# Expert results added to the token rows two at a time, and one overflow branch placed later

## The chip, the cores and the metric

The kernel runs on one core of a Trainium2 chip. The metric is the device time of one execution in microseconds (us). Before the change it is 507.67 us, the median of three runs (507.65 to 509.39).

The core has a matrix engine (PE, TensorE), with a separate row for its weight loads (PEld), a vector engine (DVE), an activation engine (ACT), GpSimd (POOL) and SyncE (SP). Each works through its own list of instructions in order and waits on semaphores. SP issues the plain transfers (DMA), POOL the indirect ones, which gather or scatter rows by a list of indices.

## The reference

Three layers follow one another on 1536 tokens of 512 numbers.

```python
# 1. attention: a band of 16 tokens to each side, and 24 block summaries per sequence -> x (1536 x 512)
# 2. mixture of 8 experts, at most one expert per token
do_compute = x @ w_skip > 0
e_idx = argmax(x[do_compute] @ w_gate); gate_w = softmax probability of e_idx
for e in range(8):                       # mask: the tokens of expert e
    y[mask] = gate_w * (relu(xc[mask] @ w1[e]) @ w2[e])
out[do_compute] = xc + y                 # the other tokens keep x
# 3. gated feed-forward layer over all tokens
gate = sigmoid(x @ w_gate2); val = x @ w_val
result = (gate * val) @ w_out
```

The tokens of an expert are known only at run time, and no token belongs to two experts.

## The kernel before

**Attention (0 to some 92 us)** writes the twelve tiles of 128 token rows to `x_d`, a table in device memory. It has 128 spare rows behind the 1536 tokens. The routing yields for each expert a list of token numbers. The attention's instructions are put in order by a planner with costs per operation; the change touches it at one place, the write of zeros into the spare rows (`("z",)`, L591).

**Experts (some 92 to 196 us).** The first 64 tokens of each expert are gathered from `x_d` into `xg` (two experts per gather, L713). For each expert e, `e_s1(e, half)` multiplies them with `w1` (L735; halves 0 and 1 use two of four weight tiles each), `e_relu` applies relu (`hs`, ACT L743 and DVE L744), `e_tr` transposes (`hTp` on PE L749, copied into `hT` by ACT L751 and DVE L752), `e_s2` multiplies with `w2` into `yp` (L768), and `e_out` scales by the gate into `ysb` (ACT L778; for the last two experts DVE L785, and ACT L784 writes the same rows into `YY`). `e_add(e)` (L791) is the indirect DMA on POOL that adds `ysb` to the token rows in `x_d`; this text calls it addition e. Slots of a list that hold no token point at spare rows. The pieces are interleaved by hand: while expert e is in `e_s1`, expert e-1 is in `e_tr` and `e_s2`.

**Overflow.** Tokens 65 to 192 of an expert have a branch of their own, `e_more(e)` (L1031): each engine loads the expert's count (`TENSOR_LOAD CNT`, L1032) and compares; if it is over 64, `o_tile` computes 128 more rows and adds them by its own indirect DMA (L899). If not, each engine jumps over that code and makes up its semaphores (L1037 for experts 0 to 5, L1043 for 6 and 7). `e_more(e)` also emits `e_s2(e)` and `e_out(e)` for experts 0 to 5; for 6 and 7 it holds the branch alone.

In between, `split_some` converts weights of the third layer piece by piece (ACT L989, L1000; DVE L987 to L1001).

**Third layer (some 196 us to the end).** SP loads tokens 0 to 511 from `x_d` into `xg` (L1104) before additions 6 and 7; the results of experts 6 and 7 for these tokens come in through a multiplication of `YY` with a one-hot matrix (`hot`, L1114, L1130). PE transposes `xg` (L1125) and adds both in `xp`; ACT and DVE split `xp` into `XH` and `XL` (L1131, L1132). Tokens 512 to 1535 are loaded after all additions (`x2t`, L1152) and transposed by `x2` (L1157). `m_s1` (L1179) and `m_s2` (L1208) are the products, 48 and 24 matrix instructions at a time. The first group of `m_s1` needs tokens 0 to 511 alone; the first `x2` transposes stand behind its first 24 instructions.

**What orders the additions.** All additions write `x_d`. The framework that tracks dependencies therefore makes each one wait for the one before, and makes the loads L1104 wait for additions 0 to 5, addition 6 for these loads, and L1152 for additions 6 and 7. POOL's DMAs take eight semaphores (`DMASW0` to `DMASW7`) in turn.

```python
        if e == E - 1:
            e_more(e - 1)          # L1057, between e_s1(7, 0) and e_tr(6)
```

Of the kernel before, what the change touches and what calls it, by code (L numbers as in the profile page):

```python
# [9 lines left out]
F32 = mybir.dt.float32  # L10
# [6 lines left out]
ALU = mybir.AluOpType  # L17
# [3 lines left out]
B, H, S, D = 2, 8, 768, 64  # L21
DM = 512
E, DF = 8, 1024
# [9 lines left out]
SLOT = 64  # L33
NOV = 11
CAP = SLOT + 128
XROWS = B * S + 128
NPT, NRE = 7, 0
LD = (19, 2)
CUT_1 = 3
# [37 lines left out]
    sm=-0.4, setup=-2.3, xw=0.2, gex=0.7, end=-0.5, xtr=-0.8, lg=-1.1, vst=0.3, ksum=0.9, pv=0.1, ex=0.1,  # L77
# [22 lines left out]
C_TOK = C_I128 + 128  # L100
C_DH = C_TOK + NT
C_DUM2 = C_DH + 1
C_DUM = C_DUM2 + 1
C_DHS = C_DUM + 1
C_DUMS = C_DHS + 1
C_ALL = C_DUMS + 1
# [8 lines left out]
def consts():  # L115
    c, a = np.zeros((128, C_ALL), np.float32), np.zeros((128, A_ALL), np.float32)
    c[:, C_ID:C_ID + 128] = np.eye(128, dtype=np.float32)
    qq = np.arange(64)[:, None]
    jj = np.arange(KW)[None, :]
    for v in range(3):  # L120
        ok = np.abs(jj - WIN - qq) < WIN
        if v == 0:
            ok &= jj >= WIN
        if v == 2:
            ok &= jj < WIN + 64
        m = np.full((64, KC), np.float32(8.0 * np.log(BLK)), np.float32)
        m[:, :KW] = np.where(ok, np.float32(0.0), np.float32(-8e9))
        a[:, A_MASK + v * KC:A_MASK + (v + 1) * KC] = np.concatenate([m, m], 0)
    for p in range(128):
        if p % 32 < 9:  # L130
            a[p, A_SEL + p % 32] = 1.0
    c[:, C_IOTA8:C_IOTA8 + 8] = np.arange(8)
    c[:, C_P] = np.arange(128)
    c[:, C_T16:C_T16 + NOV] = np.arange(NOV)
    c[:, C_TRI8:C_TRI8 + 64] = (np.arange(8)[None, :] <= np.arange(8)[:, None]).reshape(-1)
    c[:, C_THR:C_THR + 12] = CAP + 128 * np.arange(12)
    a[:, A_TRI:A_TRI + 128] = np.arange(128)[:, None] < np.arange(128)[None, :]
    a[0, A_EROW:A_EROW + 8] = -BIG
    c[:, C_I64:C_I64 + CAP] = np.arange(CAP) - BIG
    c[:, C_I128:C_I128 + 128] = np.arange(128)  # L140
    p = np.arange(128)
    c[:, C_TOK:C_TOK + NT] = 1 + p[:, None] + 128 * np.arange(NT)[None, :]
    c[:, C_DH] = p // 64 - 2
    c[:, C_DUM2] = 2 * B * S + p - (p // 64 - 2)
    c[:, C_DUM] = B * S + p + 1
    c[:, C_DHS] = -1 - p // 64
    c[:, C_DUMS] = 2 * B * S + p - (-1 - p // 64)
    return c, a


# [1 line left out]
def body(ctx: ExitStack, tc, qx, kx, vx, vtx, cst, csa, wgs, w1, w2, mgate, mval, mout, out):  # L152
    nc = tc.nc
    pe, dve, act, pool, sp = nc.tensor, nc.vector, nc.scalar, nc.gpsimd, nc.sync
    ctx.enter_context(tc.manual_schedule())
    x_d = tc.dram_tile([XROWS, DM], F32, name="x_d")
# [3 lines left out]
    C = keep.tile([128, C_ALL], F32, name="C")  # L160
# [5 lines left out]
    LS = keep.tile([128, 2 * E], F32, name="LS")  # L166
# [45 lines left out]
    Z = a1.tile([128, DM], F32, name="Z")  # L212
# [346 lines left out]
    def op(key, engine, f, *deps):  # L559
        ops[key] = (engine, COST[key[0]], f, [d for d in deps if d in ops])  # L560
# [22 lines left out]
    for b in range(B):  # L583
        for n in range(NP):
# [3 lines left out]
                op(("k", b, n), "sp", lambda b=b, n=n: load_k(b, n))  # L588
                op(("ksum", b, n), "dve", lambda b=b, n=n: ksum(b, n), ("k", b, n))
            op(("vsum", b, n), "dve", lambda b=b, n=n: vsum(b, n), ("vt", b, n))  # L590
    op(("z",), "sp", lambda: sp.dma_start(x_d[B * S:, :], Z))  # L591

    def vsums(b, *deps):
        op(("vst", b), "pe", lambda: vsum_t(b), *[("vsum", b, n) for n in range(NP)], *deps)
# [73 lines left out]
    while avail:  # L668
        best = None
        for key in avail:  # L670
            g, c, _, deps = ops[key]
            r = max((done[d] + (0.0 if ops[d][0] == g else LAT[ops[d][0]] + (LSP if g == "sp" else 0.0)) for d in deps), default=0.0)
# [4 lines left out]
        g, c = ops[key][:2]  # L677
# [27 lines left out]
    m1 = mst.enter_context(tc.tile_pool(name="m1", bufs=1, side="right"))  # L705
# [4 lines left out]
    xg = [m1.tile([128, DM], F32, name=f"xg{j}") for j in range(4)]  # L710
# [62 lines left out]
    def e_out(e):  # L773
# [13 lines left out]
        if e < E - 2:  # L787
            e_add(e)

    def e_add(e):  # L790
        pool.indirect_dma_start(  # L791
            x_h, bass.IndirectOffsetOnAxis(ap=SI[:, e:e + 1], axis=0), ysbs[e], None, compute_op=ALU.add
        )


    def o_eq(u, base, pos, p):
# [109 lines left out]
    with tc.If(nl > 0):  # L906
        with tc.For_i(0, nl, 1) as it:
# [15 lines left out]
                op=ALU.subtract,  # L923
# [33 lines left out]
        gather(j)  # L957
    dve.tensor_scalar(LI2, LS[:, E:2 * E], -1.0, 0.0, op0=ALU.add, op1=ALU.max)
    sm = m1.tile([128, E], F32, name="sm")
    dve.tensor_scalar(sm, LS[:, :E], 0.5, C[:, C_DUM2:C_DUM2 + 1], op0=ALU.is_lt, op1=ALU.mult)  # L960
    dve.scalar_tensor_tensor(sm, LS[:, :E], 2.0, sm, op0=ALU.mult, op1=ALU.add)
    dve.tensor_scalar(SI, sm, C[:, C_DH:C_DH + 1], None, op0=ALU.add)
    z = E - 1
# [55 lines left out]
    def split_some(i):  # L1019
        for _ in range(SPN[i]):  # L1020
            k = next(sp_order, None)
            if k is not None:
                next(sp0[k], None)
# [7 lines left out]
    def e_more(e):  # L1031
        rv = nc.values_load(CNT[0:1, e:e + 1], min_val=0, max_val=B * S)  # L1032
        yi, gt = SI2[:, e:e + 1], GLS[:, E + e:E + e + 1]
        if e in cuts:
            yps[e] = pB.tile([128, 512], F32, name=f"yp{e}", tag="b")
            e_s2_mm(e, range(S2N))
            with tc.If(rv > SLOT) as cmp:  # L1037
                o_tile(e, xo[e], yi, gt, cuts[e], lambda: e_s2_mm(e, range(S2N, 8)))
            with cmp.Else():
                e_s2_mm(e, range(S2N, 8))  # L1040
            e_out(e)
        else:
            with tc.If(rv > SLOT):  # L1043
                o_tile(e, xo[e], yi, gt, Cut(e, *w12(e)))
# [8 lines left out]
    for e in range(E):  # L1053
        if e + AHD < E:
            o_gather(e + AHD)
        e_s1(e, 0)
        if e == E - 1:  # L1057
            e_more(e - 1)
        if e >= 1:
            e_tr(e - 1)  # L1060
        load_to(ahead(3 * e + 1), True)
        if e == E - 2:
            split_some(1)
        e_s1(e, 1)
        if e == E - 1:
            split_some(5)
        e_relu(e)
        load_to(ahead(3 * e + 2), True)
        if e >= E - 2:
            split_some(2 if e == E - 2 else 6)  # L1070
        if e % 2 == 1 and e + 1 < E:
            g_tr((e + 1) // 2)
        if 1 <= e < E - 1:
            if e < E - 1:
                cuts[e - 1] = Cut(e - 1, *w12(e - 1), CUT_0)
                cuts[e - 1](CUT_0)
            else:
                e_s2(e - 1)
            if e == E - 2:
                split_some(3)  # L1080
            load_to(ahead(3 * e + 3), True)
            e_more(e - 1)
            if wpos >= NW:
                load_free(8 * e)
        if 8 * e >= NW > 8 * e - 8:
            xst.close()
            wpool = ctx.enter_context(tc.tile_pool(name="wpool", bufs=1, side="left"))
            rawt = ctx.enter_context(tc.tile_pool(name="rawt", bufs=RWB, side="left"))
            WHL = [(wpool.tile([128, 3072], F32R, name="wh0"), wpool.tile([128, 3072], F32R, name="wl0")), None]
        if E - 3 <= e < E - 1:  # L1090
            split_some(0 if e == E - 3 else 4)
# [9 lines left out]
    XH = [[hst.tile([128, 512], F32R, name=f"XH0_{n}", tag="wh") for n in range(4)]]  # L1101
    XL = [[hst.tile([128, 512], F32R, name=f"XL0_{n}", tag="wh") for n in range(4)]]
    for t in range(4):
        sp.dma_start(xg[t], x_d[t * 128:t * 128 + 128, :])  # L1104
    e_add(E - 2)
    TT = m1.tile([128, 2], F32, name="TT")
    dve.tensor_copy(TT[0:64, :], LS[0:64, E - 2:E])
# [40 lines left out]
    x2t = {}  # L1148

    def x2_load(t):  # L1150
        x2t[t] = z4.tile([128, DM], F32, name=f"x2t{t}", tag="x2t")
        sp.dma_start(x2t[t], x_d[t * 128:t * 128 + 128, :])  # L1152

    def x2(t):
        ps = pB.tile([128, 4, 128], F32, name=f"x2p{t}", tag="b")
# [144 lines left out]
```

## Time and profile before

| What | Value |
|---|---|
| median of three runs | 507.67 us |
| the profiled execution: its time / its span | 510.82 us / 509.0 us |
| PE busy, share of the span | 486.7 us, 96% |
| POOL busy | 107.8 us, 21% |
| chain that ended last: PE / DMA | 58% / 8% of the span |
| of it, additions `x_d<-ysb,SI` | 6% |
| granted PE clock, mean | 0.973 |

The span runs from the first to the last instruction. The chain that ended last is followed back from the last instruction: at each step to whatever released it, or to the instruction before it on its engine. PE is called busy in most slices; where it stands still is seen in the timeline, in brackets behind an instruction: the idle time before it and who ended it. Additions are counted by POOL only for the time in which it writes their descriptors (some 1.55 us); how long the data takes stands in the chain.

### The profile page before, as it was taken

What the parts mean: (1) busy time and instruction counts of PE and PEld (TensorE: products, weight loads), DVE (VectorE), ACT (ScalarE), POOL (GpSimd) and SP (SyncE); (2) the same over time, 40 slices, a digit from 0 to 9 for tenths busy, and PEclk for the clock granted to TensorE, in tenths of its full rate; (3) what the DMA queues carried; (4) which work ended last, traced back from release to release, by engine and by line L of the source; (5) the groups of instructions that cost most, each with busy time, mean ns of one, the idle gap of its engine ahead of it and who ended that gap; (6) DMA issues with size and microseconds to landing.
All of it is one profiled execution on the core that took longest, in us unless ns stands there. A gap on an engine that the chain in (4) does not pass through costs nothing.

```text
span 509.0 us, 8116 instructions
## 1 busy us (share of the span) xinstructions
PE 486.7 (96%) x2889; PEld 371.7 (73%) x2889; DVE 287.2 (56%) x813; ACT 187.2 (37%) x403; POOL 107.8 (21%) x158
## 2 busy tenths in 40 slices
PE   7989998899999978899999999999999999999997
PEld 3878884446575534688888888888888888888886
DVE  4979788216482553256865564556545574556324
ACT  2988762016481332334432323223332323322110
POOL 5654213611112121111321221112111221112000
PEclk9899997699999989899999999999999999999999
DMA  8899789999999674552222210222012210000114
GB/s 275 289 249 302 232 280 325 385 336 406 412 381 340 206 247 102 190 236 84 82 82 85 82 50 33 84 82 84 6 77 84 83 61 23 1 0 0 43 41 166
DMA packets 27483, 83.08 MB, mean 163 GB/s; under 512 B 3096, under 2 KB 5016, under 8 KB 25384
## 3 DMA queue, kind: packets, MB, share of 16 engines
q1 hardware_dynamic: 25032, 77.71, 43.2%
q0 software_dynamic: 2400, 4.72, 4.1%
q8 instruction: 28, 0.46, 0.4%
q14 instruction: 23, 0.19, 0.1%
HBM read 73.69 MB, written 8.13 MB: 161 GB/s over the span
## 4 chain that ended last, share of the span: by engine, by line
PE 58%; DMA 8%; issue 2%; SPq 0%; POOLq 0%; DVE 0%
PE s L1179 38%; PE s L1208 19%; DMA x_d<-ysb,SI 6%; PE x2p L1157 1%; DMA xg<-x_d 1%; DMA x2t<-x_d 1%; DMA x_d<-yo,SI 0%; SPq L1104 0%; POOLq L1032 0%; DVE ACC L1216 0%; POOLq L791 0%; SPq L1152 0%; POOLq L1001 0%
## 5 line engine op out<-in xcount | busy, mean ns | idle before, releaser
L1179 PE MATMUL s<-XH,wh 128*128 128x512 f32 x288 | 113.3, 394 | 0.0
L1179 PE MATMUL s<-XL,wh 128*128 128x512 f32 x288 | 112.3, 390 | 0.0
L1179 PE MATMUL s<-XH,wl 128*128 128x512 f32 x288 | 112.3, 390 | 0.0
L1001 POOL TENSOR_TENSOR wl<-x,wh 128x512 fp32r<-128x512 f32 x32 | 41.9, 1312 | 219.0 <-ACT wh L1000 214.6
L1193 DVE TENSOR_TENSOR pr<-s,sg 128x512 f32<-128x512 f32 x36 | 24.9, 691 | 89.4 <-PE s L1179 85.6
L1179 PEld LDWEIGHTS s<-XH,wh 128*128 128x128 f32 x288 | 54.4, 189 | 11.4 <-issue 0.2
L1179 PEld LDWEIGHTS s<-XL,wh 128*128 128x128 f32 x288 | 54.4, 189 | 11.3 <-DVE XL L1132 0.2
L1179 PEld LDWEIGHTS s<-XH,wl 128*128 128x128 f32 x288 | 54.2, 188 | 11.4
L1208 PE MATMUL s<-wl,GH 128*128 128x512 f32 (+1 forms) x146 | 56.4, 386 | 0.0
L1208 PE MATMUL s<-wh,GL 128*128 128x512 f32 (+1 forms) x146 | 56.4, 386 | 0.0
L1208 PE MATMUL s<-wh,GH 128*128 128x512 f32 (+1 forms) x146 | 56.4, 386 | 0.0
L1000 ACT ACTIVATE wh<-x 128x512 fp32r<-128x512 f32 x36 | 22.6, 632 | 67.2 <-DVE x L994 67.2
L1194 ACT ACTIVATE GH<-pr 128x512 fp32r<-128x512 f32 x36 | 22.7, 632 | 65.5 <-DVE pr L1193 65.5
L1216 DVE TENSOR_TENSOR ACC<-s,ACC 128x512 f32<-128x512 f32 (+1 forms) x61 | 39.1, 677 | 6.8 <-PE s L1208 6.8
L1195 DVE TENSOR_TENSOR GL<-pr,GH 128x512 fp32r<-128x512 f32 x36 | 24.9, 692 | 25.1 <-ACT GH L1194 25.1
L989 ACT ACTIVATE u<-u 128x512 f32<-128x512 f32 x36 | 22.5, 626 | 42.4 <-DVE u L987 42.3
L735 PE MATMUL hp<-wt,xgT 128*64 128x512 f32 x128 | 33.8, 659 | 0.6 <-ACT xgT L725 0.6
L345 ACT ACTIVATE P<-P,nm 128x120 f32<-128x120 f32 x96 | 29.7, 383 | 5.5 <-DVE nm L338 5.5
L1208 PEld LDWEIGHTS s<-wh,GH 128*128 128x128 f32 x146 | 27.4, 188 | 5.6
L1208 PEld LDWEIGHTS s<-wh,GL 128*128 128x128 f32 x146 | 27.4, 188 | 5.5
L1208 PEld LDWEIGHTS s<-wl,GH 128*128 128x128 f32 x146 | 27.4, 188 | 5.5
L1191 ACT ACTIVATE sg<-s 128x512 f32<-128x512 f32 x36 | 21.1, 587 | 26.0 <-PE s L1179 26.0
(186 smaller groups left out, 700.1 us busy)
## 6 DMA issues: line engine op xcount, KB each, us to landing
wt<-w SPq DMA_DIRECT2D x64, 512.0 KB, 11.3
wr<-mout SPq DMA_DIRECT2D x6, 1024.0 KB, 4.8
wr<-mgate SPq DMA_DIRECT2D x5, 1024.0 KB, 7.9
wr<-mval SPq DMA_DIRECT2D x5, 1024.0 KB, 4.8
vw<-vx SPq DMA_DIRECT2D x12, 390.0 KB, 5.9
kr<-kx SPq DMA_DIRECT2D x8, 400.0 KB
qs<-qx SPq DMA_DIRECT2D x12, 256.0 KB, 6.2
vt<-vtx SPq DMA_DIRECT2D x8, 384.0 KB, 5.0
```

The costliest lines, as they stand in the source:

```text
L345: act.activation(Pt[i][:, n, :], Pt[i][:, n, :], AF.Exp, bias=nmt[i][:, n:n + 1], scale=-1.0)
L735: pe.matmul(hp[e][c * 64:c * 64 + 64, :], xgT[e // 2][:, n, (e % 2) * 64:(e % 2) * 64 + 64], WT[2 * e, n][:, c * 512:c * 512 + 512], start ...
L989: act.activation(u, u, AF.Copy, scale=2.0 ** -112)
L1000: act.activation(hi[:, d], w, AF.Copy)
L1001: (dve if g == 0 and k < WLE else pool).tensor_tensor(lo[:, d], w, hi[:, d].bitcast(F32), op=ALU.subtract)
L1179: pe.matmul(ps, a[:, o:o + 128], x, start=k == 0, stop=k == 11)
L1191: act.activation(sg, pp[0], AF.Sigmoid)
L1193: dve.tensor_tensor(pr, pp[1], sg, op=ALU.mult)
L1194: act.activation(GH[u][:, f, :], pr, AF.Copy)
L1195: dve.tensor_tensor(GL[u][:, f, :], pr, GH[u][:, f, :].bitcast(F32), op=ALU.subtract)
L1208: pe.matmul(ps, a[u][:, f, r * 128:r * 128 + 128], b[:, o + a0:o + a1], start=k == 0, stop=k == 5)
L1216: dve.tensor_tensor(acc, ps, acc, op=ALU.add)
```

## The change

Four things are done.

1. Addition e no longer waits for addition e-1 (`declare_no_dep`); it waits for addition e-2 (`after(a, adds[-2:-1])`). The loads of tokens 0 to 511 get waits for all additions 0 to 5 by hand, those of the other tokens for additions 6 and 7. A `memset` of one column on POOL stands ahead of each addition.
2. So that two additions in flight do not share spare rows, there are 256 of them: empty slots of even experts point at the first 128, those of odd experts and of the overflow tiles at the last 128. Zeros are written by two DMAs in place of one, and one vector instruction that computes the indices (L960) becomes two of half the width.
3. `e_more(6)` moves from behind `e_s1(7, 0)` to behind `e_s1(7, 1)`.
4. A table of constants grows by one column.

```diff
-XROWS = B * S + 128
+XROWS = B * S + 256
...
-    c[:, C_DUM2] = 2 * B * S + p - (p // 64 - 2)
-    c[:, C_DUM] = B * S + p + 1
+    for j in range(2):
+        c[:, C_DUM2 + j] = 2 * B * S + 128 * j + p - (p // 64 - 2)
+    c[:, C_DUM] = B * S + 128 + p + 1
...
-    op(("z",), "sp", lambda: sp.dma_start(x_d[B * S:, :], Z))
+    op(("z",), "sp", lambda: [sp.dma_start(x_d[r:r + 128, :], Z) for r in range(B * S, XROWS, 128)])
...
+    adds = []
+    GAP = m1.tile([128, 1], F32, name="GAP")
+
+    def after(ins, others):
+        for o in others:
+            tc.add_manual_dep(
+                ins.ins, o.ins.name, mybir.DependencyInfo(mybir.DependencyClass.Sync, mybir.DependencyReason.DATA)
+            )
+        return ins
+
     def e_add(e):
-        pool.indirect_dma_start(
+        pool.memset(GAP, 0.0)
+        a = pool.indirect_dma_start(
             x_h, bass.IndirectOffsetOnAxis(ap=SI[:, e:e + 1], axis=0), ysbs[e], None, compute_op=ALU.add
         )
+        if e:
+            tc.declare_no_dep(a.ins, adds[-1].ins, reason="two experts have no token in common")
+        after(a, adds[-2:-1])
+        adds.append(a)
...
         e_s1(e, 0)
-        if e == E - 1:
-            e_more(e - 1)
         if e >= 1:
             e_tr(e - 1)
...
         e_s1(e, 1)
         if e == E - 1:
+            e_more(e - 1)
             split_some(5)
...
-        sp.dma_start(xg[t], x_d[t * 128:t * 128 + 128, :])
+        after(sp.dma_start(xg[t], x_d[t * 128:t * 128 + 128, :]), adds)
...
-        sp.dma_start(x2t[t], x_d[t * 128:t * 128 + 128, :])
+        after(sp.dma_start(x2t[t], x_d[t * 128:t * 128 + 128, :]), adds[-2:])
```

How the instructions stand, first on POOL, from addition 3 (`ysb_3054`) over the overflow branch of expert 4 to addition 4 (`ysb_3279`), before. Behind a row are the semaphores that it waits for: `DMASW1` belongs to addition 2, `DMASW3` to addition 3, `DMASW2` and `DMASW4` to the overflow additions of experts 3 and 4.

```order
L791 DMA x_d<-ysb_3054,SI 3328x256 [waits DMASW2_49,DMASW1_49,Activation_49]
L1032 TENSOR_LOAD CNT
L1037 COMPARE_AND_BRANCH
L899 DMA x_d<-yo_3263,SI_72 1664x512 [waits DMASW3_49,DVE_49]
L1037 UNCONDITIONAL_BRANCH
L1037 ISA [waits DMASW4_49]
L1037 UNCONDITIONAL_BRANCH
L791 DMA x_d<-ysb_3279,SI 3328x256 [waits DMASW4_49,DMASW3_49,Activation_49]
```

The same place on POOL after the change:

```order
L804 MEMSET GAP 128x1 [waits Pool_49]
L805 DMA x_d<-ysb_3060,SI 3584x256 [waits DMASW2_49,Activation_49]
L1053 TENSOR_LOAD CNT
L1058 COMPARE_AND_BRANCH
L917 DMA x_d<-yo_3270,SI_72 1792x512 [waits DMASW3_49,DVE_49]
L1058 UNCONDITIONAL_BRANCH
L1058 ISA [waits DMASW4_49]
L1058 UNCONDITIONAL_BRANCH
L804 MEMSET GAP 128x1 [waits Pool_49]
L805 DMA x_d<-ysb_3286,SI 3584x256 [waits DMASW4_49,DMASW1_49,Activation_49]
```

Addition 3 has lost its wait for addition 2, and addition 4 waits for addition 2 where it waited for addition 3.

On PE before, from the end of expert 6's overflow branch to the branch of expert 7 (`hTp` are the transposes `e_tr(6)`, `hp` the products `e_s1(7, 1)`):

```order
L1043 UNCONDITIONAL_BRANCH
L1043 UNCONDITIONAL_BRANCH [waits PE_49]
L749 MATMUL hTp_3730<-C,hs_3334 128x128 [waits Activation_49]
L749 MATMUL hTp_3730<-C,hs_3334 128x128 x3
L735 MATMUL hp_3560<-wt_2_3290,xgT_3082 64x512 [waits DMAHW6_49]
L735 MATMUL hp_3560<-wt_2_3290,xgT_3082 64x512
L735 MATMUL hp_3560<-wt_3_3292,xgT_3082 64x512 [waits DMAHW7_49]
L735 MATMUL hp_3560<-wt_3_3292,xgT_3082 64x512
L1032 TENSOR_LOAD CNT
L1043 COMPARE_AND_BRANCH
```

On PE after, from the products `e_s1(7, 0)` to the branch of expert 6:

```order
L736 MATMUL hp_3569<-wt_0_3294,xgT_3089 64x512 [waits DMAHW5_49,DVE_49]
L736 MATMUL hp_3569<-wt_0_3294,xgT_3089 64x512
L736 MATMUL hp_3569<-wt_1_3296,xgT_3089 64x512 [waits DMAHW6_49]
L736 MATMUL hp_3569<-wt_1_3296,xgT_3089 64x512
L750 MATMUL hTp_3574<-C,hs_3342 128x128 [waits Activation_49]
L750 MATMUL hTp_3574<-C,hs_3342 128x128 x3
L736 MATMUL hp_3569<-wt_2_3298,xgT_3089 64x512 [waits DMAHW7_49]
L736 MATMUL hp_3569<-wt_2_3298,xgT_3089 64x512
L736 MATMUL hp_3569<-wt_3_3300,xgT_3089 64x512 [waits DMAHW0_49]
L736 MATMUL hp_3569<-wt_3_3300,xgT_3089 64x512
L1053 TENSOR_LOAD CNT
L1064 COMPARE_AND_BRANCH
```

(The trace records each of the four products of `e_s1(7, 1)` as two instructions.) The transposes now stand ahead of both branches. The branches of experts 6 and 7 follow one another with nothing between them on PE, and `e_s2(6)` comes behind the second.

## Rows read from the trace of the kernel before

**Rows 1.** The page: the chain that ended last, by engine and by line.

```profile
PE 58%; DMA 8%; issue 2%; SPq 0%; POOLq 0%; DVE 0%
```

**Rows 2.** The chain in order of time, 168 to 230 us: start, duration, what.

```profile
168.60 8.05 DMA x_d<-ysb,SI
...
177.39 7.08 DMA x_d<-ysb,SI
...
185.21 4.33 DMA x_d<-ysb,SI
...
190.27 3.83 DMA x_d<-ysb,SI
...
195.63 4.33 DMA xg<-x_d
...
200.73 3.67 DMA x_d<-ysb,SI
...
205.14 3.75 DMA x_d<-ysb,SI
...
209.14 2.56 DMA x2t<-x_d
...
213.74 3.56 PE s L1179 x12
217.29 0.87 PE x2p L1157 x8
...
227.22 2.74 PE s L1179 x12
```

**Rows 3.** Timeline, ACT scaling results; in brackets idle time before, and its releaser.

```profile
163.28 0.47 ACT L778 ACTIVATE ysb<-yp,GLS 128x256 f32<-128x256 f32 x1 [3.07 <-PE yp L768]
...
171.64 0.47 ACT L778 ACTIVATE ysb<-yp,GLS 128x256 f32<-128x256 f32 x1 [3.23 <-PE yp L768]
...
182.89 0.47 ACT L778 ACTIVATE ysb<-yp,GLS 128x256 f32<-128x256 f32 x1 [0.17 <-ACTq L1037]
```

**Rows 4.** Timeline, PE from the transposes of expert 6 to the third layer.

```profile
183.42 0.66 PE L749 MATMUL hTp<-C,hs 128*128 128x128 f32 x4 [2.49 <-ACTq L1043]
...
184.00 3.14 PE L735 MATMUL hp<-wt,xgT 128*64 128x512 f32 x8
...
187.44 2.21 PE L768 MATMUL yp<-wt,hT 128*64 128x256 f32 x16 [0.30 <-PEq L1043]
...
190.16 5.40 PE L768 MATMUL yp<-wt,hT 128*64 128x256 f32 x48
...
196.93 1.36 PE L1125 MATMUL xp<-C,xg 128*128 128x128 f32 x8 [1.37 <-DMA xg<-x_d]
...
211.84 1.90 PE L1157 MATMUL x2p<-C,x2t 128*128 128x128 f32 x8 [2.28 <-DMA x2t<-x_d]
```

**Rows 5.** Line L1043: ns min/median/max, first and last start; L1032 on PE likewise.

```profile
L1032 PEldq TENSOR_LOAD <-CNT x8: 298/305/320, 105.7 to 183.5; - x8
...
L1043 PEldq COMPARE_BRANCH  x2: 222/1721/3220, 178.8 to 183.9; - x2
```

**Rows 6.** Stretches: length, busy PE, PEld, DVE, ACT, POOL, granted clock, DMA share.

```profile
184.60:188.00 3.40, 3.10 (x12) 0.71 (x10) 2.03 (x4) 1.31 (x3) 1.55 (x1) 0.50 0.81 208
...
195.56:203.53 7.97, 5.48 (x25) 3.12 (x25) 1.66 (x4) 2.39 (x5) 1.55 (x1) 1.00 0.45 137
203.53:211.84 8.31, 6.03 (x27) 4.51 (x25) 1.64 (x3) 2.42 (x4) 1.55 (x1) 1.00 0.37 86
...
211.90:215.30 3.40, 3.40 (x13) 3.01 (x14) 1.59 (x3) 1.68 (x3) 0.00 (x0) 0.50 1.00 370
```

**Rows 7.** Line L591, the write of zeros: ns, start.

```profile
L591 SPq DMA_DIRECT2D x_d<-Z x1: 1526/1526/1526, 46.2 to 46.2; - x1
```

**Rows 8.** Line L713, the first gathers on POOL, and their time to landing.

```profile
L713 POOL DMA_INDIRECT xg<-x_d,LI x4: 954/971/1186, 88.3 to 92.6; - x4
...
DMA to landing us min/median/max: 7.3/7.5/8.6
```

More of the change, by code (lines that the diff above doesn't have):

```diff
@@ L102 @@
 C_DUM2 = C_DH + 1
-C_DUM = C_DUM2 + 1
+C_DUM = C_DUM2 + 2
 C_DHS = C_DUM + 1
@@ L143, in consts @@
     c[:, C_DH] = p // 64 - 2
-    c[:, C_DUM2] = 2 * B * S + p - (p // 64 - 2)
-    c[:, C_DUM] = B * S + p + 1
+    for j in range(2):
+        c[:, C_DUM2 + j] = 2 * B * S + 128 * j + p - (p // 64 - 2)
+    c[:, C_DUM] = B * S + 128 + p + 1
     c[:, C_DHS] = -1 - p // 64
-    c[:, C_DUMS] = 2 * B * S + p - (-1 - p // 64)
+    c[:, C_DUMS] = 2 * B * S + 128 + p - (-1 - p // 64)
     return c, a
@@ L959, in body @@
     sm = m1.tile([128, E], F32, name="sm")
-    dve.tensor_scalar(sm, LS[:, :E], 0.5, C[:, C_DUM2:C_DUM2 + 1], op0=ALU.is_lt, op1=ALU.mult)
+    for j in range(2):
+        dve.tensor_scalar(
+            sm[:, j:E:2], LS[:, j:E:2], 0.5, C[:, C_DUM2 + j:C_DUM2 + j + 1], op0=ALU.is_lt, op1=ALU.mult
+        )
     dve.scalar_tensor_tensor(sm, LS[:, :E], 2.0, sm, op0=ALU.mult, op1=ALU.add)
```

## The prediction

> **What bounds the kernel now.** I read the page first. The chain that ended last is 58% PE and 8% DMA [rows 1], and 58% of a span of 509.0 us is 295 us, so the chain is PE alone from about 212 us to the end. Nothing that the change touches runs there; it can only decide when that stretch begins. Then I read the chain itself before 212 us. It is a string of transfers: additions 2 to 5, the loads of tokens 0 to 511, additions 6 and 7, the loads of tokens 512 to 1535 [rows 2]. The reader is to see that between one landing and the next issue there are always some 0.73 us (168.60 + 8.05 = 176.65, next issue 177.39), and that only the last loads hand over to PE.
>
> Third, the timeline of ACT, for what each addition could have started with. The results of experts 3, 4 and 5 are there at 163.75, 172.11 and 183.36 [rows 3]; additions 3, 4 and 5 are issued at 177.39, 185.21 and 190.27. So additions 3 and 4 are 13 us late, addition 5 is 6.9 us late, all because of the wait for the one before. Addition 2 waits for something else (the overflow rows of expert 2) and stays.
>
> Fourth, PE around the end of the experts. It runs `e_s2(6)` from 187.44 and ends `e_s2(7)` at 190.16 + 5.40 = 195.56; then it stands still twice for the loads and once more, 2.28 us, for the later tokens [rows 4]. The stretches give the sizes: from 195.56 to the start of `m_s1` at 203.53 PE is busy 5.48 of 7.97 us, so 2.49 us are waits; from 203.53 to 211.84 it is busy 6.03 of 8.31 us [rows 6]. [...]
>
> **The additions.** Addition 3 follows addition 2 on POOL. It writes descriptors for some 1.55 us, so addition 3 is issued near 168.60 + 1.55 + 0.2 = 170.4. Addition 4 waits for addition 2 (176.65) and its own result (172.11): 177.4. Addition 5 waits for addition 3 and for its result at 183.36: if addition 3 has landed by 183.3, addition 5 goes at 183.36 + 0.73 = 184.1, 6.2 us earlier than now. Addition 3 may take 12.9 us for that, where alone it took 7.08 [rows 2]. Addition 5 then lands after 3.83 to 4.33 us; I take 4.33, the flight of the one that was under way at that time [rows 2]: 188.4.
>
> **The loads of tokens 0 to 511.** Now addition 5 lands at 194.10; PE's first transposes of these tokens begin 2.83 us later, the last load is issued 1.53 us later and lands after 4.33 [rows 2, 4]. Carried over: first transposes possible at 191.3, the last load landed at 188.4 + 1.53 + 4.33 = 194.3. Both are before PE can be through with `e_s2(7)` (below), so the waits of 2.49 us go and PE itself is late next.
>
> **The move of `e_more(6)`.** Before, `e_tr(6)` began at 183.42, behind expert 6's branch and expert 5's scaling on ACT, which ended at 183.36 [rows 3, 4]. Now it stands ahead of both branches and waits for its own input alone, which ACT makes up 182.89 - 0.17 = 182.72 as its reconciliation of expert 5's branch ends [rows 3]; I take 182.8, 0.6 earlier. `e_tr(6)` takes 0.6, `e_s1(7, 1)` 3.14 us, of which the last part ran with the clock at 0.50 [rows 4, 6]; at its first four instructions' pace it is about 2.0. It ends between 185.4 (full clock) and 186.6. Then come two branches in series where one stood: the one of expert 7 cost a gap of 0.30 behind `e_s1(7, 1)`; a second is one load of the count (0.305 us) and one compare (0.222 at its quickest), with hand-over some 0.6 to 0.85 [rows 4, 5]. So `e_s2(6)` begins at 186.5 to 187.9 (187.44 now). Its length and `e_s2(7)`'s, 187.44 to 195.56, hold 8.12 us with four transposes in between; I let it shrink or grow by 0.3 for the clock. End of `e_s2(7)`: 194.3 to 196.0; I take 195.0.
>
> The compare of expert 6's branch took 3.22 us on PE, that of expert 7 0.222 [rows 5]. I take it that most of the 3.22 lay beside the wait for ACT (`e_tr(6)` was released by ACT, not by the branch [rows 4]); after the move nothing covers it. If it starts at 183.8, once PE's queue has handed out `e_s1(7, 1)`, it ends at 187.0 and `e_s2(6)` starts near 187.9: that is the upper end above. [...]
>
> **The third layer's start.** With no wait, the 5.48 us of work follow [rows 6]: `m_s1` starts at 195.0 + 5.5 = 200.5, against 203.53: 3.0 us earlier. Its first 24 instructions end at 206.5. Addition 6 goes at 194.3 + 0.77 = 195.0; addition 7 no longer waits for it, only for its result behind 195.0 and POOL: some 196.7. It lands 3.75 later at 200.4 [rows 2], the loads are issued 0.25 later and the first lands after 2.56 [rows 2]: 203.2, 3.3 us before PE wants it. The 2.28 us go, and with no stop ahead of it the fall of the clock as well, 1.85 us. Together 4.1.
>
> **The rest.** The memsets stand ahead of waits of POOL for results and landings, those of experts 6 and 7 ahead of transfers with 3.3 us of slack: nothing. Without that cover each costs one small POOL instruction, under the 0.95 us of the shortest instruction on that engine that stands here [rows 8]. The half-width index instruction is one more on DVE, under 0.3 us, ahead of the routing's last steps: 0 to 0.2. The second write of zeros is 1.53 us of SP's queue at 46 us [rows 7], between the attention's loads. Its bounds are 0, if these loads are ahead of their use, and 1.53 if they aren't; SP waits on buffers after that point, so I take 0.2. Below nothing it can't be: it does nothing that was done later before. That PE is later than I think between 183 and 195 I have kept as -0.9 to +0.7.
>
> Sum: 3.0 + 4.1 - 0.2 = 6.9 us. On the profiled execution (510.82, that is 1.8 over its span) 503.9; the median of the runs is 507.67, 3.15 lower, with the same program. I subtract the gain there: **500.8 us**. Its own range is 498.6 to 503.2. The gain is 7.8 if `e_s2(7)` ends at 194.3 and the zeros cost nothing, and 4.7 with the branch's stall (0.9) and the zeros at 1.53. I add 1.3 above: the profiled execution is 3.15 us longer than the median, and I can't say which of its waits and falls of the clock are a typical run's; below, the rivals stand in for that.
>
> **The rivals.**
>
> *The additions are served one after another.* Two in flight may share one queue and gain nothing but the 0.73 us of hand-over each. Then addition 3 lands at 176.65 + 7.08 = 183.7, addition 4 at 188.0 (4.33 more), addition 5 at 191.9 (3.83 more). The loads start 2.2 us earlier, not 5.7, first transposes possible at 194.7, the last load at 197.8. PE waits some 1 us, `m_s1` starts at 201.4 (2.1 gained); additions 6 and 7 land at 202.2 and 206.0, the later loads at 208.8 against 207.4: 1.4 us of wait and the fall of the clock stay. Gain 2.1 + 0.9 = 3.0: 504.7 us. For it: three flights of 7 to 8 us become 4 when less runs beside them. Against it: four gathers issued from 88.3 to 92.6 each landed 7.3 to 8.6 us after their issue [rows 8]; one after another at 7.5 the last would have needed 25 us or more.
>
> *PE becomes the bound at the branches.* Both compares take 3.22 us, bare and in series, behind 184. `e_s2(6)` starts near 190.8, `e_s2(7)` ends at 198.9, `m_s1` starts at 204.5: 1.0 later than now. The later loads are there in time, which still gives 4.1. Gain 3.1: 504.6 us. It turns to a loss from 5 us per branch on. For it [rows 5], against it the median of that row's two.
>
> *The change doesn't do what it says:* another wait (a buffer of `ysb`, the queue on POOL, a semaphore shared by two DMAs) holds additions 3 to 5 where they are. Gain 0 to 1: some 507.2. The order on POOL shows the wait for the addition before gone, which speaks against it.
>
> *Slower: two additions in flight disturb each other.* Both read and write small rows of `x_d`, beside the weight loads; if each takes over twice its time, the string gets longer than it was. At 2.5 times: addition 2 lands at 168.60 + 20.1 = 188.7, addition 4 goes at 189.4 and lands at 200.2 (10.8), the loads come 6.1 us later than now, and the later loads near 220.6 against 211.84: 8.8 us lost, 516 us. It decides from about a factor of 2, where loss and gain balance. The same gathers [rows 8], four in flight at 7.3 to 8.6 us, speak against it.
>
> **How the numbers follow.** Forecast 0.72, one after another 0.12, PE bound at the branches 0.09, no effect 0.04, slower 0.03. 0.5% is 2.5 us, about what a measurement of this kernel can tell from no change: faster means under 505.1. Forecast (0.70 of its 0.72) and some 0.17 of the two middle cases' 0.21 are under it, in all 0.87; within it 0.08 (0.04 of the middle cases, 0.02 of the forecast's tail, 0.02 of no effect); over it 0.05 (slower, and 0.02 for a loss that the branch or the zeros make). The range takes the forecast's range and reaches to the two middle cases: 498.6 to 505.0.
>
> **What would show it.** POOL's idle time before additions 3 and 5 named DMA of the addition before is gone; addition 3 is issued near 170, 4 near 177.4, 5 near 184; SP's loads of tokens 0 to 511 near 188.5. PE goes from `e_s2(7)` into the transposes with no wait for DMA, `m_s1` starts near 200.5, the x2 transposes follow their 24 products at once, and no stretch near 205 to 212 has a clock of 0.50. I am wrong if additions 2 and 3 fly for over 12.9 us, if PE's branch compares sum to over 4 us, or if the attention ends more than 1 us later behind the second write of zeros.

## The result and the profile after

The changed kernel takes 502.19 us (median of 11 runs, 499.41 to 503.89), the kernel before beside it 507.65 us (503.56 to 509.84). The ratio is 0.9906, with an interval of 0.9881 to 0.9930: 3.6 to 6.0 us faster. 500.8 was forecast, and a gain of 6.9. The profiled execution took 499.52 us, its span is 497.7. That of before took 510.82: the one lies 2.7 us below its kernel's median and the other 3.2 above, so a difference of the two traces, 11.3 us, must not be taken for the gain. Where times of two traces are compared below, they are counted from the moment at which the result of expert 5 is ready (180.29 us in the trace after, 183.36 before), since the part ahead of it differs from execution to execution. Lines of a view keep the trace's own times.

The page of the changed kernel, the chain that ended last; it answers to [rows 1].

```profile
PE 62%; DVE 0%; issue 0%; DVEq 0%
```

The 8% for DMA are gone: no transfer stands on the chain any more. The chain itself, start, duration, what; it answers to [rows 2].

```profile
183.51 1.95 PE yp L769 x16
...
193.27 3.44 PE xp L1150 x8
196.71 5.46 PE s L1199 x24
202.17 1.14 PE x2p L1177 x8
203.32 2.77 PE s L1199 x12
206.08 0.88 PE x2p L1177 x8
```

Between `e_s2(6)` and the second eight transposes only PE stands, without a gap. The second eight transposes of `x2` begin 25.8 us behind expert 5's result (206.08 - 180.29), before 33.9 us (217.29 - 183.36). By the timeline, whose starts are a little earlier and which is used from here on, it is 25.6 and 33.8 us. From those transposes to PE's last instruction it is 288.5 us in both traces. The additions 2 to 7 on POOL, and the results of experts 4 and 5 on ACT, which answer to [rows 3]:

```profile
164.22 1.57 POOL L805 DMA_INDIRECT x_d<-ysb,SI  x1 [6.70 <-issue]
...
166.09 1.56 POOL L805 DMA_INDIRECT x_d<-ysb,SI  x1 [0.19 <-issue]
...
169.31 1.56 POOL L805 DMA_INDIRECT x_d<-ysb,SI  x1 [1.54 <-ACT ysb L779]
...
180.57 1.96 POOL L805 DMA_INDIRECT x_d<-ysb,SI  x1 [9.58 <-ACT ysb L779]
...
193.48 1.56 POOL L805 DMA_INDIRECT x_d<-ysb,SI  x1 [10.77 <-DVE ysb L786]
...
195.34 1.56 POOL L805 DMA_INDIRECT x_d<-ysb,SI  x1 [0.19 <-issue]
```

```profile
168.56 0.47 ACT L779 ACTIVATE ysb<-yp,GLS 128x256 f32<-128x256 f32 x1 [3.23 <-PE yp L769]
...
179.82 0.47 ACT L779 ACTIVATE ysb<-yp,GLS 128x256 f32<-128x256 f32 x1 [0.17 <-ACTq L1058]
```

In brackets is who ended the wait ("issue" where the profile shows nobody; a q behind an engine's name stands for its sequencer, here at a branch): for additions 4 and 5 it is now ACT with the result, 0.3 us before the issue, and no longer the addition before. PE in the same stretch, which answers to [rows 4]:

```profile
177.54 1.08 PE L736 MATMUL hp<-wt,xgT 128*64 128x512 f32 x4 [0.54 <-DMA wt<-w]
179.74 0.66 PE L750 MATMUL hTp<-C,hs 128*128 128x128 f32 x4 [1.12 <-ACTq L1058]
180.33 1.94 PE L736 MATMUL hp<-wt,xgT 128*64 128x512 f32 x8
183.51 1.95 PE L769 MATMUL yp<-wt,hT 128*64 128x256 f32 x16 [1.25 <-DVE wl L1022]
...
185.97 5.40 PE L769 MATMUL yp<-wt,hT 128*64 128x256 f32 x48
191.31 1.97 PE L1145 MATMUL xp<-C,xg 128*128 128x128 f32 x16
...
202.12 1.20 PE L1177 MATMUL x2p<-C,x2t 128*128 128x128 f32 x8
```

The waits for `xg` and `x2t` are gone. What is left are a stop of 0.54 us for weights, one of 1.12 us ahead of `e_tr(6)`, for ACT, and 1.25 us ahead of `e_s2(6)`, where the two branches now stand. The bracket there names DVE; in e5 and e8 below the same 1.25 us is put down to PE's own sequencer at the branch, and with one branch fewer (e9) it shrinks to 0.30. Stretches, with the columns of [rows 6]:

```profile
191.31:196.14 4.83, 4.83 (x26) 3.16 (x25) 1.72 (x4) 2.39 (x5) 2.47 (x3) 1.00 0.21 41
196.14:202.12 5.98, 5.98 (x26) 4.52 (x25) 1.64 (x3) 2.43 (x4) 0.77 (x1) 1.00 0.54 120
202.12:205.92 3.80, 3.80 (x22) 3.09 (x22) 1.89 (x3) 2.14 (x4) 0.00 (x0) 1.00 0.98 331
```

PE is busy throughout and the granted clock is 1.00 in all three; before, 2.49 and 2.28 us of the first two were waits, and the clock was 0.50 behind the second wait. The compares of the two branches on PE (line 1064, which answers to line 1043 in [rows 5]; ns, min, median, max):

```profile
L1064 PEldq COMPARE_BRANCH  x2: 217/278/338, 180.5 to 182.9; - x2
```

### The profile page after: what moved, and what is told of

Its sections match the earlier page's. It is cut to its first block, busy times and chain, and to the rows that moved or that the text cites. A ratio compares the mean times of both kernels' runs of the same rounds, so it can differ in the third digit from the quotient of the medians.

```text
span 497.7 us, 8128 instructions
## 1 busy us (share of the span) xinstructions
PE 481.3 (97%) x2889; PEld 370.3 (74%) x2889; DVE 287.5 (58%) x814; ACT 187.5 (38%) x403; POOL 109.6 (22%) x166
## 4 chain that ended last, share of the span: by engine, by line
PE 62%; DVE 0%; issue 0%; DVEq 0%
PE s L1199 39%; PE s L1228 20%; PE yp L769 1%; PE x2p L1177 1%; PE xp L1150 1%; PE xp L1145 0%; DVE wl L1022 0%; PE hTp L750 0%; DVE ACC L1236 0%; DVE hT L753 0%; DVEq L1064 0%
## 5 line engine op out<-in xcount | busy, mean ns | idle before, releaser
L1199 PEld LDWEIGHTS s<-XL,wh 128*128 128x128 f32 x288 | 54.1, 188 | 11.3 <-DVE XL L1152 0.2
L736 PE MATMUL hp<-wt,xgT 128*64 128x512 f32 x128 | 30.6, 601 | 1.1 <-issue 0.6
L330 PE MATMUL S<-kw,qb 128*128 128x120 f32 x192 | 28.6, 296 | 2.9 <-DVE kw L553 2.7
```

What stands on the lines that cost most here:

```text
L330: pe.matmul(Sp[i][:, n, :], qb[t % 3][:, j, n, :], kwb[i % 3][:, n, :], start=True, stop=True)
L736: pe.matmul(hp[e][c * 64:c * 64 + 64, :], xgT[e // 2][:, n, (e % 2) * 64:(e % 2) * 64 + 64], WT[2 * e, n][:, c * 512:c * 512 + 512], start ...
L1199: pe.matmul(ps, a[:, o:o + 128], x, start=k == 0, stop=k == 11)
```

## The experiments

Ratios are to runs of the kernel before on the same chip, of medians 507.47 (e1 to e4), 506.99 (e5 to e8) and 506.91 us (e9, e11, e12).

| Kernel | median, us | ratio, interval | expert 5's result to second eight transposes, us |
|---|---|---|---|
| changed | 502.19 | 0.9906, 0.9881 to 0.9930 | 25.6 |
| e1: additions only | 500.53 | 0.9857, 0.9822 to 0.9892 | 26.6 |
| e2: move only | 505.36 | 0.9984, 0.9951 to 1.0018 | 32.9 |
| e3: four writes of zeros | 502.21 | 0.9907, 0.9875 to 0.9939 | 27.0 |
| e4: branch between | 501.85 | 0.9896, 0.9853 to 0.9938 | 25.8 |
| e7: additions 1 to 6 freed | 505.90 | 0.9983, 0.9949 to 1.0016 | 28.1 |
| e8: addition 7 freed | 504.87 | 0.9954, 0.9930 to 0.9978 | 32.8 |
| e5: conversions later | 503.52 | 0.9926, 0.9902 to 0.9950 | 31.3 |
| e6: the same, old place | 499.48 | 0.9875, 0.9837 to 0.9913 | 28.8 |
| e9: no branch 6 | 500.93 | 0.9883, 0.9849 to 0.9916 | 25.9 |
| e11: as e1 | 501.02 | 0.9902, 0.9866 to 0.9938 | 26.5 |
| e12: changed, again | 502.08 | 0.9910, 0.9879 to 0.9941 | 26.5 |

The ratio is not the quotient of the two medians (e2: 0.9984, where the medians give 0.9958). The last column is from one profiled execution each, by the timeline. In e5 and e6 expert 5's result itself comes earlier, so theirs does not compare with the others.

**e1, the additions alone.**

```diff
         e_s1(e, 0)
+        if e == E - 1:
+            e_more(e - 1)
         if e >= 1:
             e_tr(e - 1)
...
         if e == E - 1:
-            e_more(e - 1)
             split_some(5)
```

> The changed kernel with the branch of expert 6 back in its old place, between e_s1(7, 0) and e_tr(6); additions, spare rows and loads as changed. Theory (the gain is the additions' alone, the move is worth nothing or a little): 5 to 7 us faster than the kernel before, within 1 us of the changed kernel; additions 3 and 4 issued as their results are ready, no wait of PE for the loads of tokens 0 to 511 nor for the later ones, m_s1 within 1 us of where the changed kernel has it, counted from the issue of addition 2 (31.9 us). Rival 1 (the move is needed for the gain): 2 to 4 us faster only, with PE standing over 2 us at the old place of the branch. Rival 2 (the move costs, since two bare branches cost 1.25 us of PE's time): 0.5 to 1.5 us faster than the changed kernel.

It is 7.3 us faster than before (5.5 to 9.0): the additions give the whole gain, and rival 1 falls. Whether the move costs something is for e9, e11 and e12. In PE's timeline of e1 the second branch has the gap to itself:

```profile
182.36 1.12 PE L750 MATMUL hTp<-C,hs 128*128 128x128 f32 x4 [1.05 <-ACT ysb L779]
...
186.71 1.95 PE L769 MATMUL yp<-wt,hT 128*64 128x256 f32 x16 [0.31 <-PEq L1064]
```

0.31 us in place of 1.25; the other branch lies beside a wait for ACT that is there anyway.

**e2, the move alone**: the kernel before with the last two pieces of the diff of e1 turned round.

> The kernel before with the branch of expert 6 moved behind e_s1(7, 1) and nothing else changed. Theory (the gain is the additions' alone): within 1 us of the kernel before; additions 3 to 5 still one after another, PE still waits some 2.5 us for the loads of tokens 0 to 511 and some 2.3 us for the later ones, and the clock still falls behind that. Rival 1 (the move gives part of the gain): 1.5 to 3 us faster. Rival 2 (the second bare branch costs): PE's wait for the loads takes it up, so 0 in the time, and the wait in front of the first transposes gets shorter by what e_s2(7) ends later.

No difference that can be measured: the medians are 2.1 us apart, but the interval of the ratio goes from 2.5 us faster to 0.9 slower. PE of e2:

```profile
187.50 1.95 PE L768 MATMUL yp<-wt,hT 128*64 128x256 f32 x16 [1.62 <-DVEq L1043]
...
197.63 1.29 PE L1124 MATMUL xp<-C,xg 128*128 128x128 f32 x8 [0.83 <-DMA xg<-x_d]
...
210.00 1.94 PE L1156 MATMUL x2p<-C,x2t 128*128 128x128 f32 x8 [2.15 <-DMA x2t<-x_d]
```

The gap at the two branches is 1.62 us, and the wait for `xg` is 0.83 us in place of 2.45: what PE loses at the branches it would otherwise have waited for the load. The wait for `x2t` and its slow transposes (1.94 us) stay.

**e3, four writes of zeros.**

```diff
-XROWS = B * S + 256
+XROWS = B * S + 512
```

> The changed kernel with 512 spare rows, the last 256 never used, so four writes of zeros in place of two. Theory (the second write is covered by SP's waits): 0 to 0.4 us slower than the changed kernel, so 5 to 6 us faster than before. Rival (each write costs what it takes in SP's queue and pushes the attention's loads): 2 to 3 us slower than the changed kernel, so 2 to 4 us faster than before, and the first gathers of the experts start 2 to 3 us later.

502.21 against 502.19 us. The writes in SP's queue (ns min, median, max):

```profile
L592 SPq DMA_DIRECT2D x_d<-Z x4: 432/436/1266, 46.4 to 48.7; - x4
```

The writes behind the first hold SP 0.43 us each, not 1.5, and the first gather of the experts starts at 88.0 us (88.3 before, 87.4 and 87.7 in the two profiles of the changed kernel). So the term was nothing that shows. The profile of e3 shows something else: from 180 us on it runs the same instructions as the changed kernel, and yet its clock falls there.

```profile
182.00:186.00 4.00, 3.84 (x12) 0.81 (x10) 2.74 (x5) 1.91 (x5) 2.06 (x2) 0.57 0.84 270
```

PE had stood still for 1.89 us in one piece ahead of `e_tr(6)`. In the two profiles of the changed kernel that stop comes in two parts, the first for weights (0.54 and 1.12 us; 0.34 and 1.32 us in e12), and the same stretch of e12 is granted full clock:

```profile
182.00:186.00 4.00, 2.76 (x18) 1.16 (x19) 2.75 (x5) 1.92 (x4) 2.06 (x2) 1.00 0.93 309
```

Whether the stop comes in one part or two does not settle it: in e7 it is in one piece too, and the products behind it take 1.94 us, as at full clock (the clock of that trace is 1.00 from 176 to 190 us).

```profile
180.92 0.65 PE L750 MATMUL hTp<-C,hs 128*128 128x128 f32 x4 [1.89 <-ACTq L1058]
181.50 1.94 PE L736 MATMUL hp<-wt,xgT 128*64 128x512 f32 x8
```

e1 stopped in two parts (1.21 and 1.05 us) and had the fall. What decides is not shown. Where the clock falls here, `e_s1(7, 1)` takes 3.55 us in place of 1.94 (e3), so 1.6 us can come and go from one profile to the next.

**e4, the branch between `e_tr(6)` and `e_s1(7, 1)`.**

```diff
         if e >= 1:
             e_tr(e - 1)
+        if e == E - 1:
+            e_more(e - 1)
...
         if e == E - 1:
-            e_more(e - 1)
             split_some(5)
```

> The changed kernel with the branch of expert 6 one place earlier, between e_tr(6) and e_s1(7, 1), so that the two branches have 2 us of products between them. Theory (each branch costs a small bare gap, two in series 1.25 us): PE stands some 0.3 us at each, e_s2(7) ends 0.3 to 0.7 us earlier, 0 to 0.7 us faster than the changed kernel. Rival (the branch drains PE wherever it stands, and a branch between shorter pieces costs more): the same or up to 1 us slower than the changed kernel.

```profile
182.81 1.94 PE L736 MATMUL hp<-wt,xgT 128*64 128x512 f32 x8 [0.34 <-PEq L1064]
185.16 1.95 PE L769 MATMUL yp<-wt,hT 128*64 128x256 f32 x16 [0.41 <-PEq L1064]
```

Two gaps of 0.34 and 0.41 us where two branches in series left 1.25: as the theory said. In the time (501.85 us) a difference of 0.5 us cannot be seen.

**e7 and e8, which of the additions must be free.**

```diff
-        if e:
+        if 0 < e < E - 1:          # e8: if e == E - 1:
             tc.declare_no_dep(a.ins, adds[-1].ins, reason="two experts have no token in common")
-        after(a, adds[-2:-1])
+            after(a, adds[-2:-1])
```

> The changed kernel, but addition 7 waits for addition 6 again; additions 1 to 6 as changed. Theory (the whole gain comes from loads that start as expert 5's result is there; the later tokens' loads then have 2 to 3 us of slack): as the changed kernel, 5 to 6 us faster than before; addition 7 issued some 4.5 us after addition 6 and not 1.9, the later tokens' loads land 2.5 us later, and PE still doesn't wait for them, or under 0.6 us. Rival (the freed addition 7 gives the part at the later tokens, 4.1 us in the prediction): PE waits over 1.5 us for the later tokens and the clock falls, only 2 to 3 us faster than before.

> The changed kernel, but additions 1 to 6 wait for the one before again; only addition 7 doesn't wait for addition 6. Theory: PE waits some 2.5 us for the loads of tokens 0 to 511 as before, but the later tokens' loads come 2.5 us earlier against m_s1, so PE's wait for them (2.28 us) goes and the fall of the clock with it: 3 to 4.5 us faster than before. Rival (PE's wait for the first loads and the fall of the clock move on, or the second stop matters little): 0 to 1.5 us faster.

The theory fell at e7: only 0.9 us faster than before (0.8 slower to 2.6 faster). Its PE:

```profile
205.76 1.24 PE L1177 MATMUL x2p<-C,x2t 128*128 128x128 f32 x8 [2.40 <-DMA x2t<-x_d]
```

With addition 7 behind addition 6 the loads of the later tokens keep PE waiting as they did before (2.28 us). So in the trace the first half of the change needs the second: `m_s1` comes earlier, and the additions behind the loads must come earlier with it. That profile is of one of five executions of e7 at 502.3 to 503.8 us, with mean granted clocks of 0.980 to 0.986; the other seven took 505.1 to 508.1 us at 0.969 to 0.976. So the small gain of e7's median goes with the clock as well as with the wait; what the seven look like inside was not seen. e8 came out 2.3 us faster than before (1.1 to 3.5), under the 3 to 4.5 that were expected: its first stop stays, PE's later one goes.

```profile
197.84 0.66 PE L1145 MATMUL xp<-C,xg 128*128 128x128 f32 x4 [2.37 <-DMA xg<-x_d]
```

```profile
199.00:205.00 6.00, 5.70 (x16) 3.59 (x16) 0.47 (x1) 0.60 (x1) 3.00 (x3) 0.50 0.27 52
```

Here the half clock, which stood behind the second stop, stands behind the first. Each gives less than the whole. Together they give 3.2 us; by the intervals this cannot be told from the 4.8 us of the changed kernel.

**e5 and e6, the conversions.** With the additions out of the way, PE's stop ahead of `e_tr(6)` is ACT's, which has a conversion piece to do before expert 5's result. e5 moves two pieces behind that result, e6 does the same with the branch of expert 6 in its old place.

```diff
-SPN = (3, 1, 3, 3, 0, 2, 0, 2, 3, 0)
+SPN = (3, 1, 3, 1, 0, 2, 0, 4, 3, 0)
```

> The changed kernel with two conversion pieces of the fourth weight tile (DVE and ACT, lines 1008 to 1015) behind e_more(6) in place of ahead of expert 5's result, and the last two low parts behind e_more(7). Theory (with the additions out of the way PE stands at 180 to 183 us for ACT, whose conversion piece waits for DVE and a load of raw weights ahead of expert 5's result; this stop of 1.1 to 1.9 us also sets whether the clock falls): the result of expert 5 1 to 2.5 us earlier, PE's wait ahead of e_tr(6) under 0.6 us or named by the load of expert 7's weights, no stretch at 182 to 186 us with a clock near 0.5; 0.5 to 2.5 us faster than the changed kernel. Rival (the load of expert 7's first weights holds PE anyway): PE waits the same time for that load, within 0.5 us of the changed kernel.

> The same order of the conversion pieces, and the branch of expert 6 in its old place between e_s1(7, 0) and e_tr(6). Theory (the branch in the old place stands beside PE's wait for ACT, and behind e_s1(7, 1) it is bare): 0.5 to 1.5 us faster than the kernel with the same conversion pieces and the branch behind e_s1(7, 1), if PE still waits there; once that wait is gone the two are the same within 0.5 us. Rival (the moved branch is better, since e_tr(6) needn't wait for it): 0.5 to 1.5 us slower than that kernel.

The stop for ACT ahead of `e_tr(6)` goes in both (e6: 0.16 us, below), so the reading of that wait was right. The wait for expert 7's weights just ahead of it, which the rival named, stays (0.43 us in e5, 1.22 in e6, below), and e5's time did not follow. In its profile another stop stands in the middle of four transposes, with nothing in the trace that PE waits for; a stretch of half clock follows (granted 0.52 from 190 to 192 us). Around that gap, from 187.4 to 189.5 us, two packets stand in a DMA queue that the trace names `instruction`:

```profile
189.42 0.33 PE L750 MATMUL hTp<-C,hs 128*128 128x128 f32 x1 [1.75 <-issue]
```

```profile
q14 instruction: 2, 0.02, 2.1%
```

The stop does not stand at the branch but 16 products and three transposes behind it. That the 1.75 us are a fetch of instructions is a guess from the packets beside it, and no run shows it. e8 speaks against it, with such a stop of 0.82 us at the same four transposes and no instruction packet in it. e6 is at 499.48 us the lowest median of all, but its interval and those of e1 and the changed kernel overlap. It lies 4.0 us below e5, where the theory had the two within 0.5 us and the rival had e6 slower: both missed. In the traces 3.4 us stand in e5 alone, the stop of 1.75 us and the 48 products behind it, 7.09 us in place of 5.40; whether that belongs to the place of the branch is not shown. PE of e6:

```profile
177.47 1.08 PE L736 MATMUL hp<-wt,xgT 128*64 128x512 f32 x4 [1.22 <-DMA wt<-w]
178.71 0.63 PE L750 MATMUL hTp<-C,hs 128*128 128x128 f32 x4 [0.16 <-PEq L1064]
```

**e9, e11, e12: what the move costs.** e11 is e1 and e12 the changed kernel, both again and together with e9, which leaves the branch of expert 6 out:

```diff
         if e == E - 1:
-            e_more(e - 1)
             split_some(5)
```

> The changed kernel without the branch of expert 6 at all (its tokens 65 to 192 would be left out; there are none, so the output is the same). Theory (behind e_s1(7, 1) this branch stands bare in front of e_s2(6), where the trace shows 1.25 us of PE's time for two branches against 0.31 for one): PE's gap ahead of e_s2(6) 0.3 to 0.4 us, about 0.9 us faster than the changed kernel in that stretch, and 0.5 to 2 us in the whole, about the time of the kernel with the branch in its old place. Rival (the branch costs nothing in its new place, and the difference between the two places is chance): within 0.5 us of the changed kernel.

> The kernel with the additions' change and the branch of expert 6 in its old place, a second time, beside the changed kernel. Theory (the move costs about 1 us or more once the additions don't hold the third layer up): ratio to the kernel before 0.983 to 0.989, 1 to 2.5 us faster than the changed kernel in the same session. Rival (the two are the same): within 1 us of it.

> The changed kernel itself, beside the other two. Both theories: ratio to the kernel before 0.988 to 0.993; its profile shows whether the stretch of half clock near 183 us and a stop at the loads come and go in one and the same program.

PE ahead of `e_s2(6)`, first e9, then e12:

```profile
184.59 2.07 PE L769 MATMUL yp<-wt,hT 128*64 128x256 f32 x16 [0.30 <-PEq L1064]
```

```profile
185.11 1.95 PE L769 MATMUL yp<-wt,hT 128*64 128x256 f32 x16 [1.24 <-DVE wl L1022]
```

So in these traces the branch costs PE 0.94 us in its new place. In the time, e9 is 1.15 us and e11 1.06 us below e12, e1 was 1.7 below the changed kernel: all one way, but the intervals overlap. A cost of the move of about 1 us agrees with trace and medians; it is not settled by the ratios.

**e13, the kernel before, profiled again.**

> The kernel before, profiled a second time. Open is why the traces show 6 to 8 us of gain from the result of expert 5 to the second eight transposes of the third layer (33.8 us before, 25.6 to 27.0 in the changed kernel's profiles), where the medians show 5 us. Theory (the profiled execution of before was a slow one, 510.8 against a median of 507.5, and had both stretches of half clock in full): an execution near 507 us has that stretch at 31 to 32.5 us, with one of the two falls missing or shorter. Rival (the stretch is the same in every execution, and the changed kernel loses 1.5 to 2 us elsewhere): 33.5 us or more in this stretch, and what differs lies ahead of it.

It took 508.8 us, on another chip than e1 to e12, and the stretch from expert 5's result to the second eight transposes 32.7 us: between the two expectations. Both falls of the clock are there:

```profile
182.00:186.00 4.00, 3.57 (x12) 1.48 (x12) 2.87 (x5) 1.80 (x4) 0.00 (x0) 0.57 0.89 258
210.00:214.00 4.00, 4.00 (x16) 3.56 (x17) 1.98 (x3) 1.85 (x4) 0.00 (x0) 0.60 0.90 308
```

By the profiles at hand (32.7 and 33.8 against 25.6 and 26.5) the change is worth 6 to 8 us in this stretch, by the medians some 5. The rival, that the changed kernel loses the rest elsewhere, has no place behind this stretch: from the second eight transposes to the end of the span it is 291.8 to 292.1 us in every profile, before and after. The profiles of before, e2 and e8, whose additions 3 to 5 wait for each other, are of executions 3.2, 3.7 and 4.8 us over their kernels' medians (for e13 there is no median on its chip), so they may show more waiting than a typical run has; how a typical run of before looks was not seen, and this part stays open.

## Why the prediction was right, step by step

- **Additions.** Right in kind: 3, 4 and 5 go as their results are ready. Addition 4 went 5.0 us earlier than forecast (11.0 us ahead of expert 5's result, not 6.0), since addition 2 landed within 4.8 us and not 8.05. It made no difference.
- **Addition 5's flight** was the mis-sized term: 6.3 us, where 4.33 was taken. The flight is the time from issue to landing. Its stretch after, and that of addition 4 before, by which it was sized:

```profile
180.57:186.92 6.35, 5.11 (x38) 2.62 (x36) 3.00 (x6) 2.17 (x5) 2.06 (x2) 1.00 0.69 217
```

```profile
185.21:189.54 4.33, 4.03 (x22) 1.56 (x18) 1.83 (x4) 0.70 (x2) 1.54 (x1) 0.68 0.71 166
```

The mean DMA share was 0.69 against 0.71, so the share does not tell it. What the profiles show together: issued at 180.57 us this addition flies 6.35 us (the changed kernel), issued at 182.58 and 182.64 us 5.83 and 6.05 (e1, e4), and issued at 188.68 and 190.27 us 3.78 and 3.83 (e2, before). So part of an earlier issue is given back; why was not tested. The last load of tokens 0 to 511 is issued 9.0 us behind expert 5's result (189.26), against 6.6 forecast.
- **PE to the end of `e_s2(7)`.** Forecast to end 11.6 us behind expert 5's result, measured 11.1. The two branches in series took 1.25 us, against 0.6 to 0.85 forecast; the products beside them ran at full clock (1.94 us for `e_s1(7, 1)`). The 3.22 us compare did not appear. It stands in both profiles of before (e13 below) and in none of the others, e1 with the branch at the same place included (0.42 us); what makes it was not found. The rival in which PE is held by both compares falls with it. Nor does any run show the 0.9 us that the lower end of the gain (4.7) adds for a stall at the branch: the two compares took 0.22 and 0.34 us in both profiles of the changed kernel, and `e_s2(7)` ended 0.6 us earlier than forecast without that stall.

```profile
L1043 PEldq COMPARE_BRANCH  x2: 219/1720/3222, 177.6 to 182.9; - x2
```

- **`m_s1`.** Forecast 17.1 us behind expert 5's result, measured 15.9 (20.2 before): 4.3 us gained where 3.0 were forecast. PE was through with `e_s2(7)` 0.6 us earlier than forecast, and the work from there took 4.8 us where 5.5 was taken.
- **The slack of the later loads** was wrong: 3.3 us by the forecast. Issued at 199.45 and with the 2.56 us of [rows 2], they land at 202.0 (an estimate: this landing is not in the trace), and PE takes them at 202.12: 0.1 us. The chain from addition 5's landing over the loads and additions 6 and 7 came 1.9 us later than forecast, PE 1.3 us earlier, and the two met. That addition 7 waits only for addition 5 was a side note of the sum: by the forecast's own times even an addition 7 behind addition 6 would have brought these tokens some 0.5 us before PE wants them. e7 shows a wait of 2.40 us instead.
- **Rivals.** In the trace of e1 additions 2, 3 and 4 were issued at 166.39, 168.27 and 171.33 and landed at 170.27, 177.89 and 180.37. Addition 4 lands 2.5 us behind addition 3, less than the shortest flight alone (3.7 us), so they are not served strictly one after another. Additions 3 and 4 fly longer than before (9.6 and 9.0 us against 7.1 and 4.3), addition 2 shorter, and all are down 1.9 us ahead of expert 5's result: neither that rival nor the slower one had a place to cost anything. The zeros, taken at 0.2, cost nothing that shows.
- **The sum.** 6.9 was forecast; the medians differ by 5.5 (first result) and 4.8 (e12). In the traces the stretch from expert 5's result on gained more than forecast: 4.3 us to `m_s1` and 3.8 behind it, 8.1 in all against 3.0 + 4.1 = 7.1. So two errors of opposite sign stand in it. The trace's gain was put too low, and it was subtracted from a median that lies 3.15 us under the execution it was read from. No run shows the 1.85 us that the 4.1 take for the fall of the clock: the eight transposes and twelve products behind the wait took 1.90 + 3.56 us before [rows 2], and in the chain after, without the wait, they take 1.14 + 2.77, 1.55 us less. That 500.8 came within 1.4 us of 502.19 is in part luck; the mechanism, the waits that go and what PE then waits for, is what the traces show. The weak step is the subtraction: the prediction itself said that it could not tell which waits are a typical run's, and this is still open. A slip without weight: a gain of 4.7 makes the upper end of its own range 503.0, not 503.2.

## What to carry to other kernels

A chain of transfers that each wait for the last is shortened by what the results, not the transfers, allow: look first at when each result is ready. Where two chains run towards one engine (here PE through the experts, and the additions to the later loads), shortening one uses up the other's slack: here the later tokens' loads had 3.3 us to spare by the forecast and 0.1 in the trace, and each of two edits alone was worth 0.9 and 2.3 us where both gave some 5. In these traces a branch cost PE least beside a wait that it had anyway: 0.94 us bare in e12 against e9, nothing visible in e1, where PE stood 1.05 us for ACT. And a gain that is read from one execution's waits belongs to that execution; its distance from the median is an error of the forecast.

## What was not expected of the hardware

The flight of one and the same kind of scattered addition goes from 3.6 us (e2) to 9.9 (e4). In e1 it is 3.7 us at a DMA share of 0.31, 5.8 us at 0.79, 9.6 us at 0.95 and 9.0 us at 1.03, where the last two overlap. The share alone does not set it: before, it was 7.1 us at 1.02 and 8.05 at 0.81, with no other addition of its kind in flight.

The granted clock fell behind a stop of 1.89 us in one piece in e3 (to 0.53 from 184 to 186 us) and 1.88 in e9 (0.50 from 182 to 184), and behind two stops of 1.21 and 1.05 us in e1 (0.54 from 182 to 184). It stayed at 1.00 behind two stops of 0.54 and 1.12 us in the changed kernel and behind 1.89 us in one piece in e7; there not even the later wait of 2.40 us was followed by a fall (1.00 from 206 to 208 us), where 2.28 us were before (0.50). So the length of the stop alone does not decide it in these traces.

The eleven runs of the changed kernel spread over 4.5 us, and the mean granted clock goes with them, loosely: 0.983 at 499.41 us, 0.968 at 503.89.
